# A half tile of 64 rows handled as 128 in the second MoE, and another order of its last products

## The chip, the cores and the metric

One core of a Trainium2 chip. The metric is the device time of one execution in microseconds (us), the median of the runs. TensorE (PE) multiplies, with its weight loads kept apart as PEld; VectorE is DVE, ScalarE is ACT, GpSimd is POOL, SyncE is SP. SP and POOL issue the DMAs.

## The reference: attention, a dense MoE layer, and a top-2 MoE of eight experts

```
attn = softmax(q k^T / 8 + bias) v            # 2 batches x 8 heads x 576 tokens
x    = leaky(attn @ w_in) @ w_out             # 1152 tokens, 512 -> 2048 -> 512
top2 = two best of 8 experts for each token   # noisy gate
for e in range(8):                            # the second MoE
    out[rows of e] += weight * (relu(x[rows of e] @ w1[e]) @ w2[e])   # 512 -> 1024 -> 512
```

All data are float32. The kernel keeps float32 precision on TensorE by splitting each operand into a high and a low part and adding three products: high by high, low by high, high by low.

## The kernel before

The program runs three stages one behind the other: attention, the first MoE (`mm1`, `mm2`), and the second MoE. In the second MoE each expert has 320 slots (`C1`). The gate scatters token rows into a DRAM table `xs` of 8 x 320 = 2560 rows (`NSLOT`); a row is 516 floats, 512 of the token and four marks (where its earlier result lies, where its result goes, its weight). Unused slots hold a filler row, which four DMAs on SP's queue wrote during the attention (`fill`, L190).

An expert's 320 slots are three tiles, `STILES`: 128, 128 and a half tile of 64 rows. The work of expert e goes so:

- `load_x` (L482) loads the three tiles of `xs` into `row` tiles by DMAs on SP's queue, about half an expert ahead; `XR[e, t]` is the tile.
- `x_trans` (L528) turns the rows so that the 512 features lie on partitions: for each of four chunks of 128 features, one TensorE transposition of each of the three tiles. The rows are the operand that is loaded into the array, an identity is the one that is streamed. The half tile's transposition has 64 rows and a 64 x 64 identity. Expert 0 is turned in another way (`x_sel`, `x_early`), so `x_trans` runs for seven experts, 28 groups of three transpositions. A group stands between ordinary products on TensorE's queue.
- `x_split` (L536) makes the high and low parts (ACT, then DVE).
- Eight steps f follow, each with 12 products of `e_mm1` (L310), `e_relu` (ACT L555, DVE L562), and `e_mm2` (L581) with three products for each full tile and two for the half tile. The half tile's first accumulator holds 128 partitions: 64 of one product and 64 of another; `e_part` (ACT L586) copies the upper half out, and `e_sum` adds it.
- `back`: `e_sum` (DVE) adds earlier results and scales, one instruction for a full tile (L606), two for the half tile (L600, L606); `e_store` keeps the sum for later experts; `e_write` (POOL L615) scatters it into the output.

The order on each engine's queue is written by a planner (`Plan`). Every step is added with an engine, an assumed duration, the names it reads and writes, and a key (its due time). The planner always takes the engine that can go on first; among that engine's steps that could begin within 0.1 us of each other it takes the one with the smallest key. A step may begin once what it depends on has ended, plus a lag: 0.07 us for engines, 3.0 us for POOL's DMAs. `row` tiles are counted in a ring of 12 names: `part` of the last expert has the name that its tile `XR[7, 0]` had, twelve names before, and `e_write` of tile 0 reads that one. The planner's order is fixed; each engine then waits for semaphores only.

In the last step of the last expert (e = 7, f = 7) the three groups of products of `e_mm2` have keys that rise with the tile: tile 0, tile 1, half tile. After them only `back` is left.

Of the kernel before, what the change touches and what calls it, by code (L numbers as in the profile page):

```python
# [9 lines left out]
F32 = mybir.dt.float32  # L10
# [8 lines left out]
P = 128  # L19
# [4 lines left out]
E = 8  # L24
C1 = 320
CAP = 1280
ROW = DM + 4
NSLOT = E * C1
# [29 lines left out]
def token_runs(blk):  # L58

    b, t = BLOCKS[blk]  # L60
    if b is None:
        return [(0, 64, 512), (64, 64, SEQ + 512)]
    return [(0, P, b * SEQ + t * P)]


class Plan:
# [3 lines left out]
    def __init__(self, start):  # L70
        self.free = dict(start)
        self.steps = []
        self.wrote, self.read, self.last, self.ring = {}, {}, {}, {}

    def slot(self, name, n):

        i = self.ring[name] = self.ring.get(name, -1) + 1
        return name, i % n
# [53 lines left out]
class Moe:  # L132
    def __init__(self, ctx, tc, t, out):
        self.tc, self.nc = tc, tc.nc
        self.t, self.out = t, out
        self.ctx = ctx
        self.FF1 = 256 * t["w_in"].shape[0]
        self.FF2 = 256 * t["w1"].shape[1]
        self.dram = ctx.enter_context(tc.tile_pool(name="mdram", bufs=1, space=bass.MemoryType.DRAM))
        self.xs = self.dram.tile([NSLOT, ROW], F32, name="xs")  # L140
        self.ys = self.dram.tile([NSLOT + 1, DM], F32, name="ys")
        self.x2d = self.dram.tile([NTOK, DM], F32, name="x2d")
        self.wf = self.dram.tile([self.FF1 // 128, P, 1024], F32, name="wf")
        self.rows = {}
        self.cp = ctx.enter_context(tc.tile_pool(name="mconst", bufs=1))
        self.scat = []

    def steps(self, ident, zrow):

        nc, cp = self.nc, self.cp  # L150
        self.ident = ident

        def masks():
            self.tri = cp.tile([P, P], BF16, name="tri")
            self.ones = cp.tile([P, P], BF16, name="ones")
            nc.gpsimd.memset(self.ones, 1.0)
            nc.gpsimd.affine_select(out=self.tri, in_=self.ones, pattern=[[1, P]], base=0, channel_multiplier=-1,
                                    compare_op=OP.is_gt, fill=0.0)
            self.iota8 = cp.tile([P, E], F32, name="iota8")
            nc.gpsimd.iota(self.iota8, pattern=[[1, E]], base=0, channel_multiplier=0,  # L160
                           allow_small_or_imprecise_dtypes=True)
            self.tokid = cp.tile([P, NT], F32, name="tokid")
            for blk in range(NT):
                for p0, n, t0 in token_runs(blk):
                    nc.gpsimd.iota(self.tokid[p0:p0 + n, blk:blk + 1], pattern=[[0, 1]], base=t0,
                                   channel_multiplier=1, allow_small_or_imprecise_dtypes=True)
            self.run_ = cp.tile([P, E], BF16, name="run")
            nc.gpsimd.memset(self.run_, 0.0)
            self.rec = cp.tile([P, NT, 2, 4], I32, name="rec")
            nc.gpsimd.tensor_copy(self.rec[:, :, :, 0], self.tokid[:, :, None].to_broadcast([P, NT, 2]))  # L170
            self.nf = cp.tile([P, NT, 2], F32, name="nf")
            self.slot = cp.tile([P, NT, 2], F32, name="slot")
            self.sidx = cp.tile([P, NT, 2], I32, name="sidx")
            self.flag = cp.tile([1, 1], I32, name="flag")

        def loads():
            self.wg = cp.tile([P, DC, 2 * E], F32, name="wg")
            nc.sync.dma_start(self.wg, self.t["wg"])
            self.nz = cp.tile([P, NT, E], F32, name="nz")
            nc.sync.dma_start(self.nz, self.t["nz"])  # L180

        st = {}

        def zeros():
            st["z"] = z = zrow()
            nc.gpsimd.memset(z, 0.0)
            nc.gpsimd.memset(z.bitcast(I32)[:, DM + 2:DM + 3], int(BIG))
            nc.sync.dma_start(self.ys[0:1, :], z[0:1, :DM])

        def fill(i):  # L190
            x = self.xs.rearrange("(r p) c -> p r c", p=P)
            nc.sync.dma_start(x[:, 5 * i:5 * i + 5, :], st["z"][:, None, :].to_broadcast([P, 5, ROW]))

        return [masks, loads, zeros] + [lambda i=i: fill(i) for i in range(NSLOT // P // 5)]

    def pools(self):
# [285 lines left out]
    def load_x(self, e, t):  # L482
        o, n = STILES[t]
        self.XR[e, t] = r = self.row()
        o += 0 if e == "early" else e * C1
        self.nc.sync.dma_start(r[:n, :], self.xs[o:o + n, :])


# [39 lines left out]
    def x_trans(self, e, d, bank):  # L528
        self.T["x", e, d] = tp = self.bank(bank)
        for t, (o, n) in enumerate(STILES):  # L530
            self.nc.tensor.transpose(tp[:, o:o + n], self.XR[e, t][:n, d * P:(d + 1) * P], self.ident[:n, :n])

    def x_parts(self, e):
        return [x[:, :, e % 2 * C1:(e % 2 + 1) * C1] for x in self.xa]
# [100 lines left out]
    def run(self):  # L635
# [3 lines left out]
        nf1, nf2 = self.FF1 // P, self.FF2 // P  # L639
        U1 = len(GROUPS) * nf1  # L640

        def weight(n, key):

            if self.wsrc[n][4]:
                r64 = slot("wr64", 2)
                if n >= self.wpos_load:
                    add("SP", 2.9, self.load_weight, (), [], [r64], key - 20, 2.0)
                f = slot("wr", 3)
                if n not in self.stored:
                    for i, d in enumerate((.61, 1.15, 1.15)):  # L650
                        add("DVE", d, self.convert, (n, i), [r64] + [("first", 0)] * (n == 3), [f], key - 5)
                    add("SP", 1.5, self.store, (n,), [f], [], key)
            else:
                f = slot("wr", 3)
                add("SP", 1.5, self.load_weight, (), [], [f], key - 12, 2.0)
            if self.wsrc[n][:3] in self.W:
                return ("w0", 0)
            w = slot("w", 5)

            wait = [("sel", NT - 3)] if n == U1 else [("x", 0, DC - 1)] if U1 < n < U1 + 8 else []  # L660
            add("ACT", .95, self.split, (n, 0), [f] + wait, [w], key - 4)
            add("DVE", 1.15, self.split, (n, 1), [f, w] + [("first", 0)] * (n == 1), [w], key - 4)
            return w
# [77 lines left out]
        t = 0.0  # L741
# [32 lines left out]
        for g, (b0, nb, n) in enumerate(GROUPS):  # L774
            chunks = range(nb * P // n)
            tail = 4 if g else 0
            for f in range(nf1 - tail):
# [7 lines left out]
                if g == 0 and f in (10, 11, 12, 13):  # L785
                    d = f - 10
# [39 lines left out]
        def load(e, key):  # L826
            for q in range(3):
                xr[e, q] = slot("row", 12)
                add("SP", .73, self.load_x if e else self.load_marks, (e, q) if e else (q,), xsall, [xr[e, q]], key, 2.0)
# [32 lines left out]
        for e in range(E):  # L862
            for f in range(nf2):
                n = U1 + e * nf2 + f // 2 * 2
                if f % 2 == 0:
                    w1, w2 = weight(n, t), weight(n + 1, t + 3)
                h, gf = slot("h", 2), slot("g", 5)
                for part in [[d] for d in range(DC)] if e + f == 0 else [range(DC)]:
                    add("PE", .41 * len(part), self.e_mm1, (e, f, part), [w1] + [("x", e % 2, d) for d in part], [h], t)
                add("ACT", .33, self.e_relu, (e, f, 0), [h], [gf], t)  # L870
                add("DVE", .41, self.e_relu, (e, f, 1), [h, gf], [("gl", gf[1], 0)], t)
                t += 1.64
                for q in range(3):
                    add("PE", .43 if q == 2 else .65, self.e_mm2, (e, f, q), [w2, gf, ("gl", gf[1], 0)],
                        [(f"acc{q}", 0)], t + 3 + .41 * q)
                t += 1.73
                if f == 0 and e == 0:
                    load(1, t)
                    add("DVE", .1, self.overflow_flag, (0,), [("rec", 0)], [("m", 0)], t)
                    b = ("tp", 0)  # L880
                    add("PE", .1, self.overflow_flag, (1,), [("m", 0)], [b], t)
                    add("DVE", .1, self.overflow_flag, (2,), [b], [], t)
                if f == 2 and e:
                    gather(e, t)
                if f == 3 and 0 < e < E - 1:
                    load(e + 1, t)
                if f == 4 and e < E - 1:
                    trans(e + 1, t + 4)
            back(e, t)
# [573 lines left out]
```

## Time and profile before

| | us |
|---|---|
| median of three runs | 693.87 (693.21 to 694.53) |
| the profiled execution | 692.14 |
| its span | 690.3 |
| its TensorE busy time | 658.3 (95%) |
| its mean granted TensorE clock | 0.991 |

The span is what the hardware profiler covers of the profiled execution. Times of instructions are counted from the span's start. The second MoE fills the stretch from about 429 to 680 us. A busy time of TensorE is the union of instructions that overlap, since products are pipelined: the distance between two starts is what one costs.

### The profile page before, as it was taken

What the parts mean: (1) busy time and instruction counts of PE and PEld (TensorE: products, weight loads), DVE (VectorE), ACT (ScalarE), POOL (GpSimd) and SP (SyncE); (2) the same over time, 40 slices, a digit from 0 to 9 for tenths busy, and PEclk for the clock granted to TensorE, in tenths of its full rate; (3) what the DMA queues carried; (4) which work ended last, traced back from release to release, by engine and by line L of the source; (5) the groups of instructions that cost most, each with busy time, mean ns of one, the idle gap of its engine ahead of it and who ended that gap; (6) DMA issues with size and microseconds to landing.
All of it is one profiled execution on the core that took longest, in us unless ns stands there. A gap on an engine that the chain in (4) does not pass through costs nothing. (4 is left out here: it accounts for less than half of the span.)

```text
span 690.3 us, 14782 instructions
## 1 busy us (share of the span) xinstructions
PE 658.3 (95%) x5777; PEld 551.8 (80%) x5777; DVE 458.1 (66%) x1010; ACT 343.2 (50%) x657; POOL 180.6 (26%) x215
## 2 busy tenths in 40 slices
PE   6799989999999999999999999999999999999992
PEld 2477766777889988998989887888888888888881
DVE  7599877876879779846654354675656565665631
ACT  5487766677664433535554354543444434443420
POOL 7778655630000000000222003011314040413221
PEclk9999999999999999999999999999999999999997
DMA  3786942326357877623345215758576675858521
GB/s 116 212 240 167 320 144 69 89 67 195 110 169 227 243 256 223 240 89 142 112 135 191 62 47 169 243 169 245 155 223 208 182 248 153 264 165 251 154 76 40
DMA packets 41101, 117.54 MB, mean 170 GB/s; under 512 B 6084, under 2 KB 6340, under 8 KB 38978
## 3 DMA queue, kind: packets, MB, share of 16 engines
q1 hardware_dynamic: 36322, 104.41, 49.5%
q0 software_dynamic: 4560, 11.71, 5.0%
q8 instruction: 47, 0.77, 0.5%
q10 hardware_dynamic: 144, 0.41, 0.2%
q14 instruction: 28, 0.23, 0.1%
HBM read 76.98 MB, written 30.62 MB: 156 GB/s over the span
## 5 line engine op out<-in xcount | busy, mean ns | idle before, releaser
L284 DVE TENSOR_TENSOR wlo<-wr,whi 128x1024 fp32r<-128x1024 f32 x96 | 117.1, 1222 | 56.2 <-ACT whi L281 55.4
L310 PE MATMUL h<-xah,whi 128*128 128x320 f32 x384 | 120.1, 313 | 1.5 <-DVE gg L327 1.5
L281 ACT ACTIVATE whi<-wr 128x1024 fp32r<-128x1024 f32 x96 | 101.1, 1055 | 39.2 <-PE acc L581 19.5
L310 PE MATMUL h<-xal,whi 128*128 128x320 f32 x384 | 118.8, 309 | 0.1
L310 PE MATMUL h<-xah,wlo 128*128 128x320 f32 x384 | 118.4, 308 | 0.0
L1030 POOL TENSOR_SCALAR up<-wl,small 128x576 f32<-128x576 f32 x124 | 97.6, 805 | 52.7 <-PE m L1044 43.4
L581 PE MATMUL acc<-whi,g 128*128 128x512 f32 x320 | 107.1, 399 | 0.0
L615 POOL DMA_INDIRECT out<-row x24 | 35.1, 1461 | 186.7 <-DVE row L606 146.7
L555 ACT ACTIVATE g<-h 128x320 fp32r<-128x320 f32 x64 | 28.0, 438 | 103.5 <-issue 60.1
L310 PEld LDWEIGHTS h<-xah,whi 128*128 128x128 f32 x384 | 72.1, 188 | 9.0 <-DVE gg L327 2.0
L310 PEld LDWEIGHTS h<-xal,whi 128*128 128x128 f32 x384 | 72.1, 188 | 4.5 <-DVE xal L542 0.9
L581 PE MATMUL acc<-wlo,g 128*128 128x512 f32 (+1 forms) x192 | 75.6, 395 | 0.0
L471 POOL DMA_INDIRECT xs<-rows,sidx x18 | 20.2, 1120 | 210.4 <-ACT lk L324 142.4
L562 DVE SCALAR_TENSOR_TENSOR g<-h,g 128x64 fp32r<-128x64 f32 (+1 forms) x128 | 35.4, 318 | 56.6 <-ACT g L555 56.6
L310 PEld LDWEIGHTS h<-xah,wlo 128*128 128x128 f32 x384 | 72.1, 188 | 0.0
L1185 ACT ACTIVATE pts<-m 128x384 f32<-128x384 f32 (+1 forms) x108 | 50.1, 524 | 35.9 <-PE m L1177 33.1
L581 PEld LDWEIGHTS acc<-whi,g 128*128 128x128 f32 x320 | 56.7, 188 | 10.1
L1158 ACT ACTIVATE pp<-s,mn 128x576 f32<-128x576 f32 x72 | 54.9, 767 | 5.9 <-DVE mn L1145 5.9
L340 PE MATMUL acc<-whi,g 128*128 128x512 f32 x144 | 57.2, 397 | 0.0
L342 PE MATMUL acc<-whi,g 128*128 128x512 f32 x144 | 56.3, 391 | 0.5 <-DVE g L331 0.5
L341 PE MATMUL acc<-wlo,g 128*128 128x512 f32 x144 | 56.6, 393 | 0.0
L1145 DVE CUSTOM_DVE_ANT_0 s<-sc,bias 128x576 f32<-128x576 f32 x72 | 51.4, 748 | 1.5 <-PE sc L1134 1.4
(160 smaller groups left out, 1210.8 us busy)
## 6 DMA issues: line engine op xcount, KB each, us to landing
wr<-in_w SPq DMA_DIRECT2D x64, 512.0 KB, 3.8
bias<-bt SPq DMA_DIRECT2D x40, 288.0 KB, 3.3
wr<-in_w_in SPq DMA_DIRECT2D x8, 1024.0 KB, 6.9
wr<-in_w_out SPq DMA_DIRECT2D x8, 1024.0 KB, 7.1
wf<-wr SPq DMA_DIRECT2D x16, 512.0 KB, 4.9
wr<-wf SPq DMA_DIRECT2D x16, 512.0 KB, 3.4
xs<-xb SPq DMA_DIRECT2D x4, 1290.0 KB, 7.8
row<-xs SPq DMA_DIRECT2D x16, 258.0 KB, 5.9
```

Of the source, the lines that this page charges most:

```text
L281: self.nc.scalar.activation(w[0], r, AF.Copy)
L284: self.nc.vector.tensor_tensor(out=lo, in0=r, in1=hi.bitcast(F32), op=OP.subtract)
L310: self.nc.tensor.matmul(h, u[:, d, :], v[:, d, :], start=(d == 0 and i == 0), stop=(d == DC - 1 and i == 2))
L340: nc.tensor.matmul(acc, gh, whi, start=(f == 0), stop=False)
L341: nc.tensor.matmul(acc, gh, wlo, start=False, stop=False)
L342: nc.tensor.matmul(acc, gl, whi, start=False, stop=(f == self.FF1 // P - 1))
L562: self.nc.vector.scalar_tensor_tensor(gl, h[:, c], 0.0, g[:, c].bitcast(F32), op0=OP.max, op1=OP.subtract)
L581: nc.tensor.matmul(y, u, v, start=(f == 0 and i == 0), stop=(last and i == len(prods) - 1))
L1030: self.nc.gpsimd.tensor_scalar(u, w, 3.0e38, b, op0=OP.min, op1=OP.max)
L1145: self.nc.vector.tensor_tensor_reduce(out=s.rearrange("p (a b) -> p a b", a=2), in0=sc[:, :, :288], in1=bias[:, h, :].rearrange("p (a b) - ...
L1158: self.nc.scalar.activation(p[:, a * SEQ:(a + 1) * SEQ], s, AF.Exp, bias=mn[:, 0:1], scale=-1.0, accum_out=sm[:, 0, a:a + 1])
L1185: self.nc.scalar.activation(ps, self.PT[blk, c, k][:, :n, :], AF.Copy)
```

## The change

`xs` gets 64 more rows, filled by one more DMA on SP's queue ahead of the first `fill`. For experts 1 to 7 `load_x` loads 128 rows for the half tile: its own 64, and the 64 that follow in the table (the next expert's first rows, or the new rows). `x_trans` transposes 128 rows of all three tiles, with the whole identity. The half tile's result has 128 columns, of which `x_split` reads the first 64 as before. In the last step of the last expert the key of the half tile's products is lowered to below that of tile 0.

```diff
-        self.xs = self.dram.tile([NSLOT, ROW], F32, name="xs")
+        self.xs = self.dram.tile([NSLOT + 64, ROW], F32, name="xs")
...
-            x = self.xs.rearrange("(r p) c -> p r c", p=P)
+            x = self.xs[:NSLOT, :].rearrange("(r p) c -> p r c", p=P)
+            if i == 0:
+                nc.sync.dma_start(self.xs[NSLOT:, :], st["z"][:64, :])
...
         o, n = STILES[t]
         self.XR[e, t] = r = self.row()
-        o += 0 if e == "early" else e * C1
+        if e != "early":
+            o, n = o + e * C1, P
         self.nc.sync.dma_start(r[:n, :], self.xs[o:o + n, :])
...
         for t, (o, n) in enumerate(STILES):
-            self.nc.tensor.transpose(tp[:, o:o + n], self.XR[e, t][:n, d * P:(d + 1) * P], self.ident[:n, :n])
+            self.nc.tensor.transpose(tp[:, o:o + P], self.XR[e, t][:, d * P:(d + 1) * P], self.ident)
...
+                end = e == E - 1 and f == nf2 - 1
                 for q in range(3):
                     add("PE", .43 if q == 2 else .65, self.e_mm2, (e, f, q), [w2, gf, ("gl", gf[1], 0)],
-                        [(f"acc{q}", 0)], t + 3 + .41 * q)
+                        [(f"acc{q}", 0)], t + 3 + .41 * (q - 3 * (end and q == 2)))
```

## Rows read from the trace of the kernel before

**Rows 1.** The page: span, and busy time of each engine
```profile
span 690.3 us, 14782 instructions
PE 658.3 (95%) x5777; PEld 551.8 (80%) x5777; DVE 458.1 (66%) x1010; ACT 343.2 (50%) x657; POOL 180.6 (26%) x215
```

**Rows 2.** Busy time by stage: one expert, with its column names
```profile
core 0: us, PE busy (x) PEld busy (x) DVE busy (x) ACT busy (x) POOL busy (x), PEclk, DMA share, GB/s
481.60:513.00 31.40, 31.40 (x175) 27.13 (x174) 18.40 (x32) 13.53 (x21) 8.17 (x6) 1.00 0.67 200
```

**Rows 3.** Groups by form, weight loads: busy, mean ns, idle before, releaser
```profile
L531 PEld LDWEIGHTS acc<-ident,row 64*128 64x128 f32 x14 | 1.9, 136 | 2.3 <-issue 2.3
```

**Rows 4.** Timeline, one group of transpositions: start, us, engine, line, idle before
```profile
453.20 0.40 PE L581 MATMUL acc<-wlo,g 128*64 128x512 f32 x1
453.44 0.58 PE L531 MATMUL tp<-ident,row 128*128 128x128 f32 x3
453.75 0.13 PEld L531 LDWEIGHTS tp<-ident,row 64*128 64x128 f32 x1 [0.17 <-issue]
453.95 0.41 PE L310 MATMUL h<-xah,whi 128*128 128x320 f32 x1
454.20 0.31 PE L310 MATMUL h<-xal,whi 128*128 128x320 f32 x1
454.35 0.31 PE L310 MATMUL h<-xah,wlo 128*128 128x320 f32 x1
```

**Rows 5.** Timeline of TensorE, the gate's four transpositions of 128 rows
```profile
324.21 0.60 PE L361 MATMUL tp<-ident,rows 128*128 128x128 f32 x4
324.56 0.48 PE L340 MATMUL acc<-whi,g 128*128 128x512 f32 x1
324.88 0.40 PE L341 MATMUL acc<-wlo,g 128*128 128x512 f32 x1
```

**Rows 6.** Timeline of weight loads in the attention
```profile
122.08 0.30 PEld L1134 LDWEIGHTS sc<-kp,qh 64*128 64x128 f32 x4 [0.20 <-issue]
...
123.08 0.97 PEld L1177 LDWEIGHTS m<-ident,pp 128*128 128x128 f32 x9 [0.17 <-issue]
```

**Rows 7.** Timelines, DMA list and waits: the fill, expert 7's rows, the weights
```profile
69.35 0.55 SPq L192 DMA_DIRECT2D xs<-xb  x1
...
623.94 3.25 SPq L486 DMA_DIRECT2D row<-xs  x3
...
638.21 0.58 PE L531 MATMUL tp<-ident,row 128*128 128x128 f32 x3
...
row<-xs SPq DMA_DIRECT2D x16, 258.0 KB, 5.9
...
ACT whi L281 <- DMA wr<-in_w: 0.4, 1, 0.4
```

**Rows 8.** Timeline of the end: the last products, sums and writes
```profile
675.85 1.43 DVE L606 SCALAR_TENSOR_TENSOR row<-acc,row 128x512 f32<-128x512 f32 x2 [1.47 <-PE acc L581]
...
676.33 0.40 PE L581 MATMUL acc<-wlo,g 128*64 128x512 f32 x1
...
676.56 0.39 PE L581 MATMUL acc<-whi,g 128*128 128x512 f32 x1
676.88 1.01 POOL L615 DMA_INDIRECT out<-row  x1 [16.86 <-DVE row L606]
676.99 0.59 ACT L586 ACTIVATE row<-acc 64x512 f32<-64x512 f32 x1 [3.20 <-PE acc L581]
677.62 0.68 DVE L600 TENSOR_TENSOR row<-acc,row 64x512 f32<-64x512 f32 x1 [0.34 <-ACT row L586]
678.20 1.00 POOL L615 DMA_INDIRECT out<-row  x1 [0.30 <-issue]
678.34 0.74 DVE L606 SCALAR_TENSOR_TENSOR row<-row 64x512 f32<-64x512 f32 x1
679.50 0.92 POOL L615 DMA_INDIRECT out<-row  x1 [0.30 <-DVEq L896]
```

## The prediction

> **What bounds the kernel now.** I read the page first: TensorE is busy for 658.3 of 690.3 us, every other engine for at most 66% [rows 1]. That is an average over three stages, so next the busy times by stage: one expert takes 31.40 us, in which TensorE is busy for all 31.40, at a granted clock of 1.00, while DVE has 18.40, ACT 13.53 and the DMA engines a share of 0.67 [rows 2]. The waits say the same from the other side: from 430 to 676 us ACT waited for weights from a DMA once, for 0.4 us [rows 7]. So in the second MoE each us that leaves TensorE's queue leaves the span, and what other engines get is hidden as long as it isn't late.
>
> Busy is not the same as efficient, so the third view is the groups by form. Of all the weight loads in this stage one stands out: the load of 64 rows for the half tile's transposition has 2.3 us of idle time before it in 14 cases, put down to "issue", so to nothing the profile shows [rows 3]. The other 14, into the other bank, have a row with the same 2.3. That is 4.6 us in 28 groups, 0.165 each. It isn't the wait for the rows: then only the first group of an expert would have it.
>
> **The transpositions (28 groups).** The timeline of one group [rows 4]: three transpositions start at 453.44, the 64-row load comes at 453.75 after 0.17 us of idle, and the product behind them starts at 453.95. A product's start is modelled, so I measure to the second product, 454.20, and take off one step of such products, 454.35 - 454.20 = 0.15. The group costs 454.20 - 453.44 - 0.15 = 0.61 us.
>
> What would it cost with 128 rows three times? The gate has such a group, four transpositions of 128 rows, without a 64-row one [rows 5]: from 324.21 to the second product at 324.88 is 0.67; less one step of a 512-column product, 0.23 (676.33 to 676.56 in [rows 8]), 0.44 are left for four, 0.11 each. It has 128 streamed columns as the new transposition has, so the 64 extra columns are in it. Three cost 0.33. Saved: 0.61 - 0.33 = 0.28 a group, 28 x 0.28 = 7.8 us.
>
> The reason that I read from it: the array waits when the number of loaded rows changes, once on the way to 64 and once on the way back. The attention shows both directions: idle 0.20 us before its loads of 64 rows, 0.17 us before the loads of 128 that follow [rows 6]. In the group the way back lies between 453.75 and 453.95: 0.20 us, against 0.11 for a transposition. Two changes of 0.1 to 0.2 us make the 0.28. A change of columns does nothing of the kind: behind the product of 128 x 64 the first transposition starts 0.24 us later [rows 4], the step of any product.
>
> The Trainium skill, TensorEngine Tiling (Array Packing), section Key Properties, says that a change of the tiling mode, not merely of the tile, drains the engine. For rows the trace agrees (0.17 and 0.20 us); for 64 columns, which that page lists as a mode too, it shows no drain (0.24 against 0.23). The products with 64 columns stay, so the sum would be the same under either.
>
> Bounds: at least the idle time alone, 28 x 0.165 = 4.6 us, if the wider transposition eats what lies behind it; below, nothing, a rival. At most, if the 64-row transposition vanished up to a step of 0.09 ((324.56 - 324.21)/4): 28 x (0.61 - 0.27) = 9.5. I take 7.8, nearest to rows 5, which has the same instruction in the same form.
>
> **The loads.** Seven DMAs carry 64 more rows of 2064 bytes, 132 KB. At 200 GB/s [rows 2] that is 0.66 us of DMA an expert, with the DMA engines a third free. The wait would be on TensorE: expert 7's three loads are issued from 623.94 to 627.19; a load of 258 KB lands after 5.9 us, so at 633.1, and the first transposition starts at 638.21 [rows 7]. 5.1 us of cover, and of the seven experts this one has the least. If that cover were gone, each us would cost seven. Weight loads behind them on SP's queue come 0.66 us later at the worst, and ACT's waits for weights were 0.4 us in all [rows 7]. POOL's gathers of earlier results wait for the same tiles, and are needed only at the end of an expert. I take 0 (bounds 0 to +0.7 for one late start).
>
> **The extra fill.** One DMA of 132 KB on SP ahead of the first fill at 69.35 [rows 7]; it takes 0.55 us of SP's queue, in which a bias store may stand behind it. These stores feed blocks that come later. 0, bounds 0 to +0.55.
>
> **The last step.** The half tile's two products go first, so tiles 0 and 1 come 2 x 0.23 = 0.46 us later. What follows? By its keys it looks like a gain: the half tile's tail is the longest, ACT 0.59, then DVE 0.68 and 0.74, from 676.99 to 679.08, and only then the last write [rows 8]. If tile 1 were last, one sum of 0.72 (half of 1.43) and the write would remain: 676.95 + 0.04 + 0.72 + 0.31 = 678.02 against 679.50, a gain of 1.5.
>
> Two things take it away. First, the order of `back` isn't touched. In the planner `e_part` has the row name of XR[7, 0], which tile 0's write reads, so it comes 3.0 us after that write, far behind the sums of tiles 0 and 1. DVE's order stays: tile 0, tile 1, half tile. (The chip doesn't wait for that: `e_part` started at 676.99, while the write had started at 676.88 and takes 1.01.) So DVE starts at 675.85 + 0.46 = 676.31, works without a gap for 1.43 + 0.68 + 0.74 and three joints of 0.04, and ends at 679.28, against 679.08. ACT's copy goes under it.
>
> Second, POOL. Its three writes start at 676.88, 678.20 and 679.50: 1.32 and 1.30 apart, 1.0 of work and 0.30 of issue each [rows 8]. The second had its sum at 677.28 and the third at 679.08, 0.42 before its start where the first started 0.31 behind its sum; so POOL, not DVE, sets the last start by 0.1. A chain of three that begins 0.46 later ends 0.46 later: 677.34, 678.65, 679.96. DVE's 679.28 + 0.31 = 679.59 is earlier. Cost: +0.46. Whatever follows the last write is as before.
>
> **Sum.** -7.8 + 0.46 = -7.3 us. The profiled execution's own 692.14 becomes 684.8. It lies 1.7 below the median of the runs, so I carry the difference over: 693.87 - 7.3 = 686.5 us.
>
> **Rivals.**
>
> 1. Only the idle time goes, the wider transposition costs the rest: -4.6 + 0.46, 689.7. For it: idle time is all the profile prints. Against it: rows 5, where 128 columns cost 0.11. Chance 0.07.
> 2. The change doesn't do what it says: the stall is of the third transposition, not of its rows, and only the tail's 0.46 is left: 694.3. Against it: four transpositions in a row have none [rows 5], and the attention stalls where rows change [rows 6]. Chance 0.05. The Trainium skill, TensorE: Matmul & The Clock Gate, section Why this matters for your kernels, says that a single product over few rows takes as long as one over 128, the gain lying in several at once: by that, too, the time would be 694.3. Rows 4 against rows 5 speak against it here: the group with 64 rows is dearer.
> 3. The end goes differently: the half tile's sum first on DVE. ACT from 675.6, DVE's two to 677.7, first write 678.0, third 678.0 + 2.62 = 680.6, so +1.1 instead of +0.46: 687.2. Chance 0.04. Or tile 1 last with POOL free: -1.5, 684.6. Chance 0.03.
> 4. Slower: the half tile's load lands too late. Its place is the first transposition of each expert; it decides from a landing 5.1 us later than now, and eats the gain at 5.1 + 7.3/7 = 6.1 us later, some 12 us in all. At 13: 7.1 - 5.1 = 2.0 us in seven experts, 14 - 7.3 = +6.7, 700.6. For it: SP's queue is in order, and expert 7's three issues took 3.25 us. Against it: 132 KB are 0.66 us. Chance 0.03.
>
> **How the numbers follow.** The forecast has 0.78, with a range of its own from 685.0 to 688.0 (0.23 to 0.31 a group, and 0.7 either way as the runs scatter). The first rival and the end's variants are faster as well: 0.78 + 0.07 + 0.07 = 0.92. Within 0.2%, 1.4 us, which is about what can be told from no change, is the second, 0.05; slower the fourth, 0.03. The range reaches from the end's better variant, 684.6, to the first rival, 689.8, and leaves out 0.08 and part of the scatter.
>
> **What would show it.** In the changed kernel all 84 of the transpositions' weight loads are of 128 rows with no idle time before the third; a group costs 0.33 us by the same subtraction; an expert takes 31.4 - 1.1 = 30.3 us, TensorE still busy throughout. In the end the half tile's products stand ahead, DVE's order is unchanged, the three writes are 1.3 apart, and the last starts 3.0 us behind the last product's end (2.55 now). I am wrong if the third load keeps its idle time, if TensorE waits ahead of a first transposition, or if an expert is shorter and the span isn't.

## The result, and the profile after

The changed kernel takes 686.42 us (median of six runs, 683.14 to 689.21) against 694.17 for the kernel before in the same rounds. The ratio is 0.9887, with a 95% interval from 0.9861 to 0.9913: 7.8 us less, between 6.0 and 9.6. The forecast was 686.5, 7.3 less than the 693.87 it started from. One of the twelve runs of the kernel with the order alone, told below, took 1075.90 us at a granted clock of 0.558, the other eleven 691.40 to 696.09, and its ratio leaves that one out.

The profiled execution of the changed kernel took 689.21 us, the longest of its six. Set beside the 692.14 of the profile before it shows only 2.9 us, so the first thing to ask is in which stage the two differ. The page (busy time of each engine) of the changed kernel:

```profile
span 687.5 us, 14783 instructions
PE 654.7 (95%) x5777; PEld 553.0 (80%) x5777; DVE 458.0 (67%) x1010; ACT 342.9 (50%) x657; POOL 180.9 (26%) x215
```

TensorE's timeline has a landmark in both: the first transposition of expert 1. It starts at 450.35 before and at 455.44 after, so the changed kernel was already 5.1 us *behind* before the first instruction that the change speeds up. The busy times of the first 60 us show where the larger part comes from; first the kernel before, then the changed one (span of the stretch, TensorE's busy time with its instructions, granted clock, DMA share, GB/s):

```profile
0.00:60.00 60.00, 48.46 (x652) 0.97 0.69 194
```

```profile
0.00:60.00 60.00, 48.07 (x586) 0.91 0.64 182
```

Fewer instructions at a lower granted clock, 0.91 against 0.97 of full speed, in a stretch in which nothing of the change has run: the extra fill is issued at 72.63. At 60 us the same product starts 3.3 us later than before. By 240 us the lag is down to 2.5, and the stretch from 250 to 300 us, where the granted clock is 0.97 against 1.00, brings it to 5.1. The extra fill isn't the cause: the kernel with the half tile twice running, told below, has neither it nor wider loads, and it shows the same 0.91 and 0.97 in these stretches and the landmark at 455.80. In six other kernels with the wider transpositions or loads, told below, the same landmark lies between 449.5 and 452.6. So the 5.1 us belong to this execution, and the stages after it are compared from landmark to landmark.

From the first transposition of expert 1 to the first one of expert 7 are 24 groups: 187.86 us before (638.21 - 450.35), 180.84 after (636.28 - 455.44). That is 7.02 us, 0.29 a group. One expert with its granted clock, for [rows 2]:

```profile
485.50:515.90 30.40, 30.40 (x176) 27.09 (x175) 18.40 (x32) 13.54 (x21) 8.39 (x6) 1.00 0.72 211
```

TensorE is still busy throughout. The line's 30.40 us and the 31.40 of [rows 2] are stretches a little wider than one expert. From the first transposition of one expert to that of the next it is 31.31 us before (187.86/6) and 30.14 after (180.84/6), 1.17 less. The groups by form of the weight loads, for [rows 3]: a form with 64 rows no longer exists, and the idle time put down to "issue" is gone.

```profile
L534 PEld LDWEIGHTS acc<-ident,row 128*128 128x128 f32 x42 | 5.4, 140 | 1.0
```

One group in TensorE's timeline, for [rows 4]:

```profile
457.73 0.39 PE L584 MATMUL acc<-wlo,g 128*64 128x512 f32 x1
457.96 0.49 PE L534 MATMUL tp<-ident,row 128*128 128x128 f32 x3
458.20 0.39 PE L312 MATMUL h<-xah,whi 128*128 128x320 f32 x1
458.43 0.31 PE L312 MATMUL h<-xal,whi 128*128 128x320 f32 x1
458.58 0.31 PE L312 MATMUL h<-xah,wlo 128*128 128x320 f32 x1
```

By the same subtraction the group costs 458.43 - 457.96 - 0.15 = 0.32 us, where it cost 0.61.

The end, for [rows 8], ACT, DVE, POOL and TensorE's last products:

```profile
672.51 0.59 ACT L589 ACTIVATE row<-acc 64x512 f32<-64x512 f32 x1 [1.82 <-PE acc L584]
673.21 1.44 DVE L609 SCALAR_TENSOR_TENSOR row<-acc,row 128x512 f32<-128x512 f32 x2 [1.93 <-PE acc L584]
673.24 0.62 PE L584 MATMUL acc<-whi,g 128*128 128x512 f32 x2
674.24 1.01 POOL L618 DMA_INDIRECT out<-row  x1 [17.32 <-DVE row L609]
674.57 0.67 DVE L603 TENSOR_TENSOR row<-acc,row 64x512 f32<-64x512 f32 x1
675.27 0.74 DVE L609 SCALAR_TENSOR_TENSOR row<-row 64x512 f32<-64x512 f32 x1
675.55 1.34 POOL L618 DMA_INDIRECT out<-row  x1 [0.30 <-DVE row L603]
677.20 0.92 POOL L618 DMA_INDIRECT out<-row  x1 [0.30 <-issue]
```

The last product ends at 673.24 + 0.62 = 673.86. The last write starts 3.34 us behind it; before it was 679.50 - 676.95 = 2.55, and 3.0 was forecast. DVE's order is unchanged, and ACT's copy is done early. The new thing is the second write: 1.34 us, where each of the others takes 0.92 to 1.01.

### The profile page after: what moved, and what is told of

Read it like the earlier page. It is cut to its first block, busy times and chain, and to the rows that moved or that the text cites. A ratio compares the mean times of both kernels' runs of the same rounds, so it can differ in the third digit from the quotient of the medians.

```text
span 687.5 us, 14783 instructions
## 1 busy us (share of the span) xinstructions
PE 654.7 (95%) x5777; PEld 553.0 (80%) x5777; DVE 458.0 (67%) x1010; ACT 342.9 (50%) x657; POOL 180.9 (26%) x215
## 4 chain that ended last, share of the span: by engine, by line
PE 79%; DVE 9%; DMA 5%; ACT 3%; issue 2%; POOL 0%; DVEq 0%; ACTq 0%; POOLq 0%
PE h L312 28%; PE acc L584 17%; PE m L1206 5%; PE sc L1138 5%; PE m L1181 4%; PE m L1048 4%; PE acc L344 4%; PE acc L342 3%; PE acc L343 3%; DMA wr<-in_w_in 3%; ACT pts L1189 2%; PE acc L523 1%; DMA wr<-in_w_out 1%; PE acc L380 1%; PE sc L1048 1%
```

## The experiments

Theory: TensorE stalls where the number of loaded rows changes, and the wider transposition takes two such changes out of each of 28 groups; the new order of the end costs a little, by POOL's chain of three writes. The rivals are named run by run.

**The rows alone.** The changed kernel with the old key:

```diff
-                        [(f"acc{q}", 0)], t + 3 + .41 * (q - 3 * (end and q == 2)))
+                        [(f"acc{q}", 0)], t + 3 + .41 * q)
```

> The rows alone, with the last step in its old order. Theory (each change of the number of loaded rows stalls TensorE, and the new order of the end costs): a group of three transpositions costs 0.33 us as in the changed kernel, and the last write starts 2.5 to 2.6 us behind the end of the last product, as before; time 7.8 us below the kernel before, 0.5 to 0.8 below the changed one. Rival (the new order of the end gains): the time is above the changed kernel's by up to 1.5 us.

Measured: 684.52 us (six runs), ratio to the kernel before 0.9868 (0.9838 to 0.9899). Expert 1 to expert 7 takes 180.83 us. Its end, POOL's writes:

```profile
668.27 1.01 POOL L618 DMA_INDIRECT out<-row  x1 [16.86 <-DVE row L609]
669.59 1.00 POOL L618 DMA_INDIRECT out<-row  x1 [0.30 <-issue]
670.89 0.92 POOL L618 DMA_INDIRECT out<-row  x1 [0.30 <-DVEq L900]
```

The last product ends at 668.34, so the last write starts 2.55 behind it, as before. The rows carry the whole gain; that the order gains is out. By time this kernel and the changed one can't be told apart.

**The order alone.** The kernel before with the new key:

```diff
+                end = e == E - 1 and f == nf2 - 1
...
-                        [(f"acc{q}", 0)], t + 3 + .41 * q)
+                        [(f"acc{q}", 0)], t + 3 + .41 * (q - 3 * (end and q == 2)))
```

> The order of the last step alone. Theory: groups of transpositions cost 0.61 us as before; the half tile's products stand first, DVE's order stays, and the last write starts 3.0 to 3.3 us behind the last product's end instead of 2.55; time 0.5 to 0.8 us above the kernel before, which the timing can hardly tell from none. Rival (the order gains): the last write starts 1.1 us behind the last product's end, 1.5 us less.

Measured: 694.36 us (median of twelve runs) beside 694.47, ratio 0.9987 (0.9965 to 1.0009); 187.86 us from expert 1 to expert 7, as before. POOL's last two writes:

```profile
681.05 1.34 POOL L615 DMA_INDIRECT out<-row  x1 [0.30 <-DVE row L600]
682.70 0.92 POOL L615 DMA_INDIRECT out<-row  x1 [0.30 <-issue]
```

The last product ends at 679.36: again 3.34 us, and again a second write of 1.34. The pattern of the end comes back to a hundredth, so it belongs to the order and not to one execution. The timing can't tell its cost from none.

**The loads alone.** The rows-only kernel with the old transpositions:

```diff
-            self.nc.tensor.transpose(tp[:, o:o + P], self.XR[e, t][:, d * P:(d + 1) * P], self.ident)
+            self.nc.tensor.transpose(tp[:, o:o + n], self.XR[e, t][:n, d * P:(d + 1) * P], self.ident[:n, :n])
```

> The loads alone: the table with 64 more rows, the extra fill and the half tile's loads of 128 rows, but transpositions of 64 rows and the old order of the end. Theory (the loads are hidden): groups cost 0.61 us with 0.17 us of idle time before the 64-row load, TensorE never waits for a first transposition, and from the first transposition to the last it is 193.7 us as before. Rival (the wider load is late): idle time before the first transposition of an expert, put down to a DMA.

Measured: from the first transposition of expert 1 (450.29) to that of expert 7 (638.15) it is 187.86 us, to the hundredth as before, and the idle time is back. The weight loads by form:

```profile
L534 PEld LDWEIGHTS acc<-ident,row 64*128 64x128 f32 x14 | 1.9, 136 | 2.3 <-issue 2.3
```

The wider loads are hidden and gain nothing by themselves. (The one run took 691.93 us, the kernel before 691.06 to 695.80 beside it.)

**The half tile twice running, and the half tile in between.** Two kernels that add work to the kernel before, the same transpositions in another order:

```diff
-        for t, (o, n) in enumerate(STILES):
+        for t in (0, 1, 2, 2):      # the other kernel: (2, 0, 2, 1)
+            o, n = STILES[t]
```

> The kernel before, but each group transposes its half tile of 64 rows twice running (128, 128, 64, 64 rows; the second repeats the first). Theory (a stall at each change of the number of rows, 0.14 us each way, and 0.11 for any transposition): 4 x 0.11 + 2 x 0.14 = 0.72 us a group, and idle time before one of the two 64-row loads only. Rival (every load of 64 rows costs 0.39): 2 x 0.11 + 2 x 0.39 = 1.00 us, idle time before both.

> The kernel before, but each group transposes 64, 128, 64, 128 rows (the half tile first and again in the middle). The same four transpositions as in the run with the half tile twice running, with four changes of the number of rows instead of two. Theory (stall at each change): 4 x 0.11 + 4 x 0.14 = 1.00 us a group, and idle time before both 64-row loads. Rival (a fixed price of a 64-row load): 1.00 us as well, so that only the pair of runs tells them apart: 0.72 and 1.00 for the theory, 1.00 and 1.00 for the rival.

TensorE's timeline of one group with the half tile twice running:

```profile
459.01 0.65 PE L532 MATMUL tp<-ident,row 128*128 128x128 f32 x4
459.59 0.41 PE L310 MATMUL h<-xah,whi 128*128 128x320 f32 x1
459.84 0.31 PE L310 MATMUL h<-xal,whi 128*128 128x320 f32 x1
```

The two 64-row loads of that group are one row, with idle time before the first of them only:

```profile
459.32 0.20 PEld L532 LDWEIGHTS tp<-ident,row 64*128 64x128 f32 x2 [0.17 <-issue]
```

And TensorE's timeline with the half tile in between:

```profile
453.68 0.40 PE L582 MATMUL acc<-wlo,g 128*64 128x512 f32 x1
454.01 1.00 PE L532 MATMUL tp<-ident,row 64*128 64x64 f32 x4
454.76 0.39 PE L310 MATMUL h<-xah,whi 128*128 128x320 f32 x1
454.99 0.31 PE L310 MATMUL h<-xal,whi 128*128 128x320 f32 x1
```

Twice running: 459.84 - 459.01 - 0.15 = 0.68 us (0.72 was expected). In between, the stall comes ahead of the first transposition, so the group begins where the product before it lets go, one step of 0.23 after 453.68, at 453.91: 454.99 - 453.91 - 0.15 = 0.93 (1.00 expected). The same four transpositions cost 0.25 us more with four changes of rows than with two, about 0.12 a change; a second half tile with no change costs 0.07, less than a full one. Over 24 groups, from expert 1 to expert 7, it is 189.27 against 195.17 us, 0.25 a group as well. A fixed price of a 64-row load, 1.00 in both, is out.

The 64-row loads by form, into one of the two banks, twice running and then in between:

```profile
L532 PEld LDWEIGHTS acc<-ident,row 64*128 64x128 f32 x28 | 2.8, 137 | 2.3 <-issue 2.3
```

```profile
L532 PEld LDWEIGHTS acc<-ident,row 64*128 64x128 f32 x28 | 3.8, 136 | 5.6 <-issue 2.6 <-DVE xal L543 1.3
```

Twice running, the idle time of 28 such loads is that of 14 before the change [rows 3]; in between, it is more than twice that, which fits idle time before both, as was expected. Part of it is put down to a split on DVE, but a group starts some 0.1 us late whether DVE or "issue" is named before it.

**Expert 0 treated the same.** The rows-only kernel, and:

```diff
-        if e != "early":
-            o, n = o + e * C1, P
+        o, n = o + (0 if e == "early" else e * C1), P
...
-            self.nc.tensor.matmul(self.T["x", 0, d][:, o:o + n], self.XR["early", q][:n, d * P:(d + 1) * P],
-                                  self.ident[:n, :n], start=False, stop=False)
+            self.nc.tensor.matmul(self.T["x", 0, d][:, o:o + n], self.XR["early", q][:, d * P:(d + 1) * P],
+                                  self.ident[:, :n], start=False, stop=False)
```

> The rows alone (old order of the end), and expert 0 treated the same: its early half tile is loaded and multiplied with 128 rows and 64 columns of the identity, in four groups of plain products. Theory (the stall belongs to the change of rows, in plain products too): the 24 instructions, which took 4.06 us, take 0.7 to 1.1 us less; time 0.7 to 1.1 us below the rows-only kernel, 8.5 to 9.3 below the kernel before. Rival (plain products hide it): the 24 take as long as before.

TensorE's timeline, the kernel before and then this one:

```profile
419.40 4.06 PE L525 MATMUL acc<-ident,row 128*128 128x128 f32 x24
423.39 0.54 PE L520 MATMUL acc<-g,rows 128*128 128x320 f32 x1
```

```profile
419.90 2.87 PE L527 MATMUL acc<-ident,row 128*128 128x128 f32 x24
422.61 0.49 PE L522 MATMUL acc<-g,rows 128*128 128x320 f32 x1
```

From the first of the 24 to the product behind them: 3.99 us before, 2.71 here, 1.28 less, more than the 0.7 to 1.1 expected. The 24 instructions are four groups of three products, two instructions each, so eight changes of rows are gone, 0.16 a change. Here the streamed columns stay 64 and only the rows change, so it is the rows. Plain products don't hide it. By time, 684.94 us (ratio 0.9877, 0.9847 to 0.9908), it is faster than the kernel before and not to be told from the rows-only kernel; by its stages it should be the fastest of all that ran.

**Two writes at the end.** The changed kernel; tile 0 of the last expert isn't written.

```diff
     def e_write(self, e, t):
+        if e == E - 1 and t == 0:
+            return
```

> The changed kernel, but the last expert's tile 0 is not written to the output (its 128 rows of the output keep what they had), so POOL has two writes at the end instead of three. Theory (POOL's chain of three sets the last start): the last write starts 0.3 us behind the half tile's sum, 2.5 us behind the last product's end instead of 3.34. Rival (DVE's chain or the half tile's sum sets it): it stays at 3.2 to 3.4.

The end on POOL and DVE; the last product ends at 669.54:

```profile
670.61 1.01 POOL L620 DMA_INDIRECT out<-row  x1 [18.00 <-DVE row L609]
670.96 0.74 DVE L609 SCALAR_TENSOR_TENSOR row<-row 64x512 f32<-64x512 f32 x1
671.98 0.93 POOL L620 DMA_INDIRECT out<-row  x1 [0.36 <-DVEq L902]
```

The last write starts 2.44 us behind the last product, 0.28 behind the half tile's sum. With one write fewer DVE sets it; with three POOL does.

**The half tile's sum first.** The changed kernel, with the planner freed to sum the half tile first:

```diff
-                    part = slot("row", 12)
+                    part = slot("row", 12) if e < E - 1 else ("part", 0)
...
-                r = slot("row", 12)
-                add("DVE", 1.2 if q == 2 else .6, self.e_sum, (e, q), reads, [r], key)
+                r = slot("row", 12) if e < E - 1 or q < 2 else ("y2", 0)
+                add("DVE", 1.2 if q == 2 else .6, self.e_sum, (e, q), reads, [r], key - (e == E - 1 and q == 2))
```

> The changed kernel, with the half tile's sums also first on DVE at the end, and its write first on POOL. Theory (POOL's chain of three starts with the first sum that is done): the first write starts near 1.0 us behind the last product's end instead of 0.4, the last 3.6 to 4.0 behind it instead of 3.34. Rival (the half tile's long tail sets the end, so that taking it first gains): the last write starts 1.1 to 2.0 behind it.

Its writes; the last product ends at 671.06:

```profile
672.08 0.94 POOL L618 DMA_INDIRECT out<-row  x1 [17.95 <-DVE row L609]
...
674.64 0.98 POOL L618 DMA_INDIRECT out<-row  x1 [0.31 <-issue]
```

The first starts 1.02 us behind the last product, the last 3.58. The chain begins later and ends later; that the half tile's long tail sets the end is out. The size is just below what was expected, since here no write takes 1.34.

**Another form of the half tile's sum.** What makes the second write long? In the changed kernel it starts at 675.55, while DVE's last instruction, whose two tensors both lie in SBUF, has been running since 675.27. In the kernel before, the write starts first, at 678.20, DVE's instruction at 678.34, and the write takes 1.00 [rows 8]. The changed kernel with the operands exchanged:

```diff
             part = self.R["part", e][:n, :DM]
+            if e:
+                w = xr[:n, DM + 3:DM + 4]
+                self.nc.vector.scalar_tensor_tensor(part, part, w, self.PV[e, t][:n, :DM], op0=OP.mult, op1=OP.add)
+                self.R["y", e, t] = r = self.row()
+                self.nc.vector.scalar_tensor_tensor(r[:n, :DM], acc[:n, :], w, part, op0=OP.mult, op1=OP.add)
+                return
             self.nc.vector.tensor_tensor(out=part, in0=acc[:n, :], in1=part, op=OP.add)
             acc = part
```

> The changed kernel, with the half tile's two sums in another form for experts 1 to 7: first the copied half is scaled and the earlier result added (both in SBUF), then the accumulator from PSUM. The last instruction on DVE has one operand in SBUF instead of two. Theory (POOL's second write takes 1.34 us instead of 1.00 because it starts while a DVE instruction with two operands in SBUF is running): the second write takes 1.0 us and the last write starts 3.0 us behind the last product's end instead of 3.34, as was forecast. Rival (the second write is long for another reason, such as what the other engines do at the program's end): it takes 1.34 us and the last starts at 3.34 again.

Its end on DVE and POOL; the last product ends at 668.04:

```profile
668.42 1.01 POOL L624 DMA_INDIRECT out<-row  x1 [18.41 <-DVE row L615]
668.75 0.73 DVE L605 SCALAR_TENSOR_TENSOR row<-row 64x512 f32<-64x512 f32 x1
669.52 0.74 DVE L607 SCALAR_TENSOR_TENSOR row<-acc,row 64x512 f32<-64x512 f32 x1
669.74 1.00 POOL L624 DMA_INDIRECT out<-row  x1 [0.30 <-DVE row L605]
671.04 0.92 POOL L624 DMA_INDIRECT out<-row  x1 [0.30 <-issue]
```

The second write takes 1.00 us, and the last starts 3.00 behind the last product, the forecast's number. It starts while DVE is at work here too (669.52), but with one operand in SBUF. And an instruction with two operands in SBUF runs beside the first write (668.75), but that write had started before it and isn't longer. The rival, something at the program's end, is out.

## Why the prediction was right, step by step

**The bound** held: what left TensorE's queue in the second MoE left the stage, and TensorE stayed busy for all of it.

**The transpositions**: 0.28 us a group was forecast from the gate's groups, 0.29 measured; 28 groups at 7.02/24 are 8.2 instead of 7.8. The reading of the cause held as well. Twice running against in between shows that the change of rows is what costs, and expert 0 shows it for plain products with the columns kept. The first rival (only the printed idle time, 4.6 us) failed, because the way back, for which the profile prints no idle time in these groups, costs about as much: 0.29 less the 0.165 printed is about 0.13, and the pair of runs gives about 0.12 a change. Of the two pages of the Trainium skill that the prediction weighed, the pair of runs agrees in rows with TensorEngine Tiling (Array Packing), section Key Properties; the sentence on few rows in TensorE: Matmul & The Clock Gate, section Why this matters for your kernels, does not carry over to a product between others of 128 rows (0.61 us against 0.32 a group).

Two readings of the prediction need putting right. The page says that the ends of products are modelled, not their starts; to measure to the second product behind a group is right all the same, since the first step there is longer than the usual 0.15 (0.25 us before, 0.23 after). And of columns the trace shows only that 64 of them cost nothing (0.24 us to the next start against a step of 0.23). In the attention the loads ahead of the 64-row ones of [rows 6] have 32 columns, and a load of 32 columns behind one of 128 has idle time too, with 128 rows in both (put down to POOL there):

```profile
121.65 0.24 PEld L1202 LDWEIGHTS m<-pts,v 128*32 128x32 f32 x8
...
124.32 0.64 PEld L1044 LDWEIGHTS m<-up,small 128*32 128x32 f32 x16 [0.17 <-POOL up L1030]
```

So the first line of [rows 6] can't tell rows from columns, and only its second, 0.17 on the way back from 64 rows, speaks for rows alone. Whether a change to 32 columns stalls was not tried.

**The loads and the fill** at nothing: shown for the loads (187.86 us with them and without). Expert 7's loads are issued at 622.00 and its transpositions start at 636.28 without a wait. For the fill nothing was seen; it wasn't tried by itself.

**The last step** was right in sign and mechanism, and too small. The order of DVE, ACT's copy out of the way, and POOL's chain as the bound stood as forecast; the runs with two writes and with the half tile's sum first show the chain. Mis-sized is the term "three writes 1.3 apart, +0.46": the last write starts 0.79 us later. The missing 0.33 is the second write's 1.34, and the exchange of operands gives it back. I took a write's duration as fixed, where it depends on what DVE is doing as it starts (1.34 us beside two operands in SBUF, 1.00 beside one).

How much of it reaches the span? From the last product's end to the end of the span it is 13.35 us before and 13.36 with the rows alone, 13.64 and 13.74 with the new order (the changed kernel, and the order alone), and 13.76 with the operands exchanged. With two writes it is 13.16, with the half tile's sum first 14.04. So 0.3 to 0.4 of the 0.79 arrives, and the 0.33 that the exchange wins at the last write isn't seen at the end. "Whatever follows the last write is as before" did not hold: from the last write's start to the end of the span it is 10.8 us before, 10.3 in the changed kernel and 10.8 with the exchange. What takes up the difference stays open. The sum by stages is -8.2 + 0.3 = -7.9, beside the -7.8 of the runs.

**The carry to the median** worked, though the profile of one execution differed from that of another by 5 us in stretches that the change doesn't touch. That 686.5 lies within 0.1 of the measured 686.42 is luck: the runs give the gain only to between 6.0 and 9.6, the two terms were too small a gain by 0.4 and too large a loss by 0.2, and the kernel before came out 0.3 above the base. The range doesn't follow from its own terms at the upper end: 0.23 a group and 0.7 of scatter reach to 688.6, not 688.0.

## What to carry to other kernels

A short transposition or product among full ones can cost more than a full one: compare the whole group, from the start to the second instruction behind it, with a group that has no short member, and pad the rows if the data that come with them are harmless. A reordered end is worth what the chain of its last engine allows, here three writes of 1.3 us, and that chain starts with the first result and not with the longest tail. Before a gain is read from two profiles, find a landmark ahead of the change and take off what was there already.

## What the runs showed of the hardware that was not expected

A POOL write that starts while DVE is working on two operands in SBUF takes longer, and ends 0.8 to 0.9 us behind the end of DVE's work. The writes of all experts, minimum, median and maximum of the duration in ns, before and then with the operands exchanged:

```profile
L615 POOL DMA_INDIRECT out<-row x24: 917/1158/2627, 462.2 to 679.5; - x24
```

```profile
L624 POOL DMA_INDIRECT out<-row x24: 918/1011/1369, 460.3 to 671.0; - x24
```

Six of the 24 took 2.62 us before, the second write of experts 1 to 6. DVE and POOL in expert 1, before and then with the operands exchanged:

```profile
494.74 0.74 DVE L606 SCALAR_TENSOR_TENSOR row<-row 64x512 f32<-64x512 f32 x1
494.88 2.62 POOL L615 DMA_INDIRECT out<-row  x1 [0.31 <-DVE row L600]
495.41 1.21 DVE L284 TENSOR_TENSOR wlo<-wr,whi 128x1024 fp32r<-128x1024 f32 x1
```

```profile
491.81 1.00 POOL L624 DMA_INDIRECT out<-row  x1 [0.31 <-DVE row L605]
491.81 0.74 DVE L607 SCALAR_TENSOR_TENSOR row<-acc,row 64x512 f32<-64x512 f32 x1
492.48 1.21 DVE L286 TENSOR_TENSOR wlo<-wr,whi 128x1024 fp32r<-128x1024 f32 x1
493.12 1.37 POOL L624 DMA_INDIRECT out<-row  x1 [0.30 <-issue]
```

Before, the split of the next weights (L284), which has two operands in SBUF as well, follows the half tile's last sum at once, and the write lasts until 0.88 us behind the split's end (496.62). After the exchange the second write takes 1.00; the maximum of 1.37 is now the third one's, which starts beside such a split (it took 1.21 before, also beside one). All of these are under TensorE's work and cost nothing there. The Trainium skill, SBUF - State Buffer, section Who interferes with whom, says that a DVE instruction with two SBUF inputs contends with a GpSimd instruction that reads SBUF, and that the one issued first blocks the other. The trace agrees where DVE came first (1.34 against 1.00 us). Where POOL came first, DVE's instruction was not held up: 0.74 us beside a running write [rows 8], as long as with none running when it starts (494.74). There the measurement differs from the page.
